# The last group of tokens: all first products, then the sums token block by token block; and the bias slabs ahead of the first weights

## The chip, the cores and the metric

The kernel runs on one core of one Trainium2 chip. The core has a matrix engine (TensorE, PE in the profile; its weight loads are a row of their own, PEld), a vector engine (DVE), an activation engine (ACT), GpSimd (POOL) and SyncE (SP), which in this kernel issues all transfers. The metric is device time in microseconds; less is better.

## The reference, cut to what matters

```python
# attention: B, H, S, D = 2, 8, 768, 64; keys kept: the first n_global = 8 and the last n_local = 96
scores = q @ k.T / sqrt(D) - slope[h] * dist        # dist depends on query - key alone
a = softmax(where(keep, scores, -1e9));  x = (a @ v) as (1536 tokens, 512)
# layer 0: 512 -> 2048 -> 512
h = x @ w_in;   g = max(h, 0) + log1p(exp(-|h|));   x = g @ w_out
# layer 1: 512 -> 2048 -> 512
h = x @ w_in;   g = h * clip(h + 3, 0, 6) / 6;      out = g @ w_out
```

The weights come in 64-bit floats; the result is 32-bit.

## The kernel before, in words

**Split products.** Every product of the two layers is made of three matmuls on a high and a low part of both factors (`matmul3`: low by high, high by low, high by high, in that order). So each weight and each activation exists as a pair (`wh`, `wl`; `gh`, `gl`; `xsh`, `xsl`).

**Weights.** The hidden dimension of 2048 is cut into 16 chunks of 128 for each layer. A chunk has two units, its slice of `w_in` and its slice of `w_out`, each a transfer of 512 KB (`unit_load`, L121) and a conversion to the pair (`unit_convert`): an absolute value on ACT (L140), a clamp on POOL (L143), three bit operations on DVE (L144, L147, L148), a copy that rounds to the high part (L103 on POOL beside the attention, L105 on ACT later) and a difference on DVE (L153). A converted chunk lives in one of 11 slots of four tiles; `weight_step(m)` loads ahead and converts the next m units.

**Attention.** It is done in 24 pairs k (12 blocks of 128 queries, half of the heads at a time). `att_s(k)` loads the block's q, k and v when it begins one, makes the scores on PE (L481), adds the bias and finds the row maxima on DVE (L487), takes the exponentials on ACT (L492), and scales rows on POOL (L380, after L377 and L378 on DVE). `att_t` transposes on PE (L513) and copies back on ACT (L515); `att_v` multiplies by v on PE (L531) and, when a block is complete, splits it into `xsh` and `xsl` (L538 on ACT, L539 on DVE). The scores alternate over two pairs of PSUM banks for the first five pairs.

**The bias.** For each head there is a slab of three parts of 128 by 128, made from `far`. The third part (the block's own diagonal, all that k = 0 and k = 1 use) is made by eight ACT instructions (L446); the first two parts, which the pairs from k = 2 on use too, by `bias_of(h)` on DVE (L449), one instruction for each head. A pair needs the slabs of four heads: even k heads 0 to 3, odd k heads 4 to 7.

**The start.** A loop over p = 0 to 4 issues `att_s` three pairs ahead, `att_v`, some matmuls on zeros (`warm_up`), `att_t` and weight units. Then `layers.run` interleaves the remaining pairs with the first phase of layer 0 (`half`): halves of 24 matmuls alternate between `hf` (first products) and `accf` (second products), each 128 by 256.

**The phases.** Each layer is done in phases of 6, 5 and 5 chunks; each phase goes over three groups of 512 tokens (G), and in a group over its chunks. `item` makes one chunk of one group: 12 matmuls of 512 columns for `h`, the activation (`split_g`: in layer 1 ACT L190, DVE L191, ACT L192, DVE L193), then for each of the four blocks m of 128 tokens three matmuls into `acc[m]`, a PSUM bank. After the last chunk of the last phase DVE adds each bank, times 1/6, to `part` (L305) and SP writes 128 rows of the result (L308, 256 KB).

**Order of instructions.** The framework plans the order on each engine by its own costs; an instruction that goes through `keep_in_program_order` is pinned behind the one traced before it on its engine. Pinned are all of PE's matmuls up to the end of the first phase, the ACT instruction L140 of a unit during that time, and every `bias_of`. SP issues in its planned order, and an issue that must wait holds those behind it.

**A second path.** `check_step` looks over q and k for values out of range (24 steps, spread over the last phase), and sets `flag`. Each engine loads it at the end (L759) and branches on it (L760) past a general path that does not run with these inputs.

Of the kernel before, what the change touches and what calls it, by code (L numbers as in the profile page):

```python
# [51 lines left out]
class Layers:  # L52
# [116 lines left out]

    def split_g(self, layer, hf, n):  # L170

        nc, mp = self.nc, self.mp
        gh = mp.tile([P, 512], F32R, tag="gh", name=f"gh{n}")
        gl = mp.tile([P, 512], F32R, tag="gl", name=f"gl{n}")
        t1 = self.tp.tile([P, 512], F32, tag="t", name=f"t1{n}")
# [88 lines left out]
    def item(self, layer, ph, G, s):  # L264
# [17 lines left out]
        for m in range(4):  # L282
# [23 lines left out]
            if last_ph:  # L306
                t0 = G * GB + m * P
                nc.sync.dma_start(out=self.out[t0:t0 + P, :], in_=pm)  # L308

    def release(self, layer, ph, chunks):  # L310
        base = layer * NCH + sum(PHASES[layer][:ph])
        self.free += [self.slot[base + s] for s in chunks]
# [5 lines left out]
    def run(self, att=None, spare_step=lambda: None):  # L318
# [34 lines left out]
        for layer in range(2):  # L353
            for ph, chunks in enumerate(PHASES[layer]):
                if layer == 0 and ph == 0:
                    continue
                for G in range(T // GB):
                    for s in range(chunks):
                        self.item(layer, ph, G, s)
                        if G == T // GB - 1:  # L360
                            self.release(layer, ph, (s,))
                        self.weight_step(2)
                        if layer == 1 and ph == len(PHASES[1]) - 1:
                            spare_step()
                            spare_step()
# [17 lines left out]
def fast_path(tc, ident, nf, counts, q, k, qt, kt, v, weights, out, flag):  # L383


    with ExitStack() as ctx, ExitStack() as actx:
# [60 lines left out]

        def bias_of(h):
            tc.keep_in_program_order(nc.vector.tensor_scalar(  # L449
                out=bias[:, h, 0:2, :], in0=far[:, 0:2, :], scalar1=-SLOPES[h] / SCALE, scalar2=None, op0=ALU.mult  # L450
            ))

# [3 lines left out]
        def att_s(k):  # L456
# [28 lines left out]
            for z in range(4):  # L485
# [5 lines left out]
                )  # L491
                nc.scalar.activation(pmz, pmz, AF.Exp, bias=nm[:, z:z + 1], scale=-1.0, accum_out=sm[:, z:z + 1])  # L492
            rs = ap_m.tile([P, 4], F32, tag="rs", name=f"rs{k}")
            softmax_rows(nc, sm, rs, [pm[:, z, 0:w] for z in range(4)])
# [122 lines left out]
        for p in range(LEAD):  # L617
            while step["s"] < min(p + AHEAD, quads):
                if step["s"] == 2:
                    layers.weight_step(1)  # L620
                    for h in range(H):
                        bias_of(h)
                att_step("s")
            att_step("v", p - V_LAG + 1)
            warm_up(FILL[p])
            for _ in range(2):
                att_step("t")
            layers.weight_step(LEAD_UNITS[p] - (p == 0))
        layers.run(Att, check_step)
# [178 lines left out]
```

## Time and profile before

| | us |
|---|---|
| time, median of 3 runs (lowest, highest) | 659.28 (657.86, 660.02) |
| the profiled execution: its time | 659.89 |
| the profiled execution: its span, from first to last instruction | 657.6 |
| TensorE busy in that span | 628.1 |
| DVE, ACT, POOL busy | 429.8, 375.4, 148.5 |
| mean granted TensorE clock | 0.988 |

The span is what the trace covers; the time includes 2.29 us around it. Busy times of different engines overlap.

### The profile page before, as it was taken

Reading aid. Unit: us, or ns where it says so; the run is one execution under the profiler, and the core shown is the slowest. Engines: PE = TensorE matmul, PEld = TensorE weight load, DVE = VectorE, ACT = ScalarE, POOL = GpSimd, SP = SyncE. Lnnn points to the kernel's source line nnn. Section 1 sums busy time; section 2 is a strip of 40 time slices with the busy share of each in tenths; the row PEclk is TensorE's granted clock in tenths of the full one; section 3 lists DMA queues with packets and bytes.
Section 4 is the critical chain, followed back from the end, with each engine's and each line's share of the span. In section 5 each row is a group of like instructions: output and inputs, shape, how many; then the busy total and the mean of one; then the engine's idle time right before and its main releaser. Section 6 shows DMA issues by size and latency. Waiting matters only on the chain.

```text
span 657.6 us, 9611 instructions
## 1 busy us (share of the span) xinstructions
PE 628.1 (96%) x3481; PEld 514.6 (78%) x3481; DVE 429.8 (65%) x902; ACT 375.4 (57%) x786; POOL 148.5 (23%) x192
## 2 busy tenths in 40 slices
PE   8587998999999999999999999999999999999995
PEld 4366887889999888877788888888877888888874
DVE  5897568654789999999998995225832333424242
ACT  5577778775587977867687852325675222212220
POOL 3575454531024132625200420000100000000000
PEclk9698999999999999999999999999999999999999
DMA  8452331101035233433311132000473000001011
GB/s 281 168 201 87 116 97 53 37 21 70 33 98 160 96 129 104 136 113 112 129 48 52 46 129 96 1 1 32 118 219 81 0 1 0 1 1 64 1 65 69
DMA packets 24937, 53.67 MB, mean 82 GB/s; under 512 B 2480, under 2 KB 8880, under 8 KB 24880
## 3 DMA queue, kind: packets, MB, share of 16 engines
q1 hardware_dynamic: 24880, 52.96, 24.8%
q8 instruction: 29, 0.48, 0.3%
q14 instruction: 28, 0.23, 0.1%
HBM read 49.81 MB, written 3.15 MB: 81 GB/s over the span
## 4 chain that ended last, share of the span: by engine, by line
PE 62%; DVE 19%; ACT 6%; DMA 4%; POOL 4%; issue 3%; SPq 0%; ACTq 0%; POOLq 0%; DVEq 0%
PE acc L201 22%; PE h L201 22%; PE accf L201 6%; PE hf L201 5%; DMA chk<-in_q 3%; DVE wa L147 2%; DVE wa L148 2%; POOL pm L380 2%; DVE w L153 2%; ACT pm L492 2%; PE ptp L513 2%; DVE pm L487 2%; PE s L481 2%; POOL wa L143 1%; DVE gl L193 1%
## 5 line engine op out<-in xcount | busy, mean ns | idle before, releaser
L201 PE MATMUL h<-xsh,w 128*128 128x512 f32 x624 | 170.3, 396 | 0.4 <-DVE t L187 0.4
L201 PEld LDWEIGHTS h<-xsh,w 128*128 128x128 f32 x624 | 116.7, 188 | 29.5 <-DVE t L187 1.6
L143 POOL TENSOR_SCALAR wa<-wa 128x512 f32<-128x512 f32 x56 | 76.3, 1368 | 240.2 <-ACT wa L140 239.9
L201 PE MATMUL acc<-w,gh 128*128 128x512 f32 x384 | 120.6, 395 | 0.0
L191 DVE SCALAR_TENSOR_TENSOR t<-t,h 128x512 f32<-128x512 f32 x48 | 32.9, 686 | 96.7 <-ACT t L190 96.7
L190 ACT ACTIVATE t<-h,three 128x512 f32<-128x512 f32 x48 | 33.0, 687 | 105.2 <-PE h L201 105.1
L201 PE MATMUL h<-xsl,w 128*128 128x512 f32 x312 | 87.8, 396 | 0.0
L193 DVE TENSOR_TENSOR gl<-t,gh 128x512 fp32r<-128x512 f32 x78 | 55.2, 708 | 47.3 <-ACT gh L192 47.0
L201 PEld LDWEIGHTS acc<-w,gh 128*128 128x128 f32 x384 | 72.0, 188 | 17.4
L201 PE MATMUL acc<-gh,w 128*128 128x512 f32 x240 | 78.9, 396 | 0.3 <-DVE part L297 0.2
L201 PE MATMUL acc<-w,gl 128*128 128x512 f32 x192 | 76.3, 397 | 0.8 <-ACT part L303 0.4
L192 ACT CAST gh<-t 128x512 fp32r<-128x512 f32 x78 | 48.3, 619 | 50.3 <-PE acc L201 24.3
L201 PEld LDWEIGHTS h<-xsl,w 128*128 128x128 f32 x312 | 58.5, 188 | 14.1
L380 POOL TENSOR_SCALAR pm<-pm,rs 128x256 f32<-128x256 f32 (+1 forms) x96 | 51.0, 549 | 44.5 <-DVE rs L378 33.2
L201 PE MATMUL accf<-ghf,w 128*128 128x256 f32 x288 | 59.6, 291 | 0.6 <-ACT ghf L192 0.6
L492 ACT ACTIVATE pm<-pm,nm 128x256 f32<-128x256 f32 (+1 forms) x96 | 46.0, 480 | 16.5 <-DVE nm L487 16.3
L201 PEld LDWEIGHTS acc<-gh,w 128*128 128x128 f32 x240 | 44.9, 188 | 11.9 <-DVE part L297 0.6
L201 PEld LDWEIGHTS accf<-ghf,w 128*128 128x128 f32 x288 | 47.3, 191 | 2.2 <-issue 1.2
L201 PE MATMUL acc<-gl,w 128*128 128x512 f32 x120 | 47.5, 396 | 0.0
L153 DVE TENSOR_TENSOR w<-wa,w 128x512 fp32r<-128x512 f32 x56 | 38.9, 696 | 9.2 <-ACT w L105 8.3
L201 PE MATMUL hf<-xsh,w 128*128 128x256 f32 x288 | 44.8, 286 | 0.0
L201 PEld LDWEIGHTS acc<-w,gl 128*128 128x128 f32 x192 | 36.0, 188 | 11.0 <-DVE gl L193 1.7
(105 smaller groups left out, 989.2 us busy)
## 6 DMA issues: line engine op xcount, KB each, us to landing
raw<-in_w2i SPq DMA_DIRECT2D x16, 512.0 KB, 3.3
raw<-in_w2o SPq DMA_DIRECT2D x16, 512.0 KB, 3.3
raw<-in_w1i SPq DMA_DIRECT2D x14, 512.0 KB, 3.6
raw<-in_w1o SPq DMA_DIRECT2D x12, 512.0 KB, 3.3
V<-in_v SPq DMA_DIRECT2D x12, 256.0 KB, 2.9
chk<-in_q SPq DMA_DIRECT2D x12, 256.0 KB, 3.3
chk<-in_k SPq DMA_DIRECT2D x12, 256.0 KB, 2.8
out_x<-part SPq DMA_DIRECT2D x12, 256.0 KB, 2.1
```

What stands on the lines that cost most here:

```text
L143: nc.gpsimd.tensor_scalar(out=a, in0=a, scalar1=W_HI, scalar2=W_LO, op0=ALU.min, op1=ALU.max)
L147: nc.vector.scalar_tensor_tensor(out=ai, in0=hi, scalar=-2 ** 30, in1=ai, op0=ALU.bitwise_and, op1=ALU.bitwise_or)
L148: nc.vector.scalar_tensor_tensor(out=ai, in0=lo, scalar=29, in1=ai, op0=ALU.logical_shift_right, op1=ALU.bitwise_or)
L153: nc.vector.tensor_tensor(out=wl, in0=a, in1=r32(wh), op=ALU.subtract)
L190: nc.scalar.activation(t1, hf, AF.Relu, bias=self.three[:, 0:1])
L191: nc.vector.scalar_tensor_tensor(out=t3, in0=t1, scalar=6.0, in1=hf, op0=ALU.min, op1=ALU.mult)
L192: nc.scalar.copy(gh, t3)
L193: nc.vector.tensor_tensor(out=gl, in0=t3, in1=r32(gh), op=ALU.subtract)
L201: return self.nc.tensor.matmul(out, lhsT=a, rhs=b, start=start and z == 0, stop=stop and z == len(seq) - 1, **kw)
L380: nc.gpsimd.tensor_scalar(out=t, in0=t, scalar1=rs[:, j:j + 1], scalar2=0.0, op0=ALU.mult, op1=ALU.add)
L481: layers.ordered(lambda: nc.tensor.matmul(ps[j][:, a, 0:nsl, :], lhsT=qT[n][hp, 2 * e + a, :], rhs=kT[hp, 2 * e + a, ks, :], start=True, s ...
L492: nc.scalar.activation(pmz, pmz, AF.Exp, bias=nm[:, z:z + 1], scale=-1.0, accum_out=sm[:, z:z + 1])
```

## The change

Two things are changed. In the start, `bias_of` takes a range of heads: heads 0 to 3 are done as soon as `far` exists, heads 4 to 7 inside `att_s(0)` behind its four L487, and the third pair's `att_s` no longer has a weight unit and eight `bias_of` in front of it; both units of p = 0 come at the end of p = 0. In the last phase of layer 1, the last group no longer goes through `item`: `last_items` makes the `h` and `g` of all five chunks first (the pairs of `g` in a free weight slot, two of its four tiles), and then for each block m of 128 tokens all five chunks' matmuls, the addition and the transfer; the last block in two halves of 256 columns. The remaining four `check_step` calls come behind the first chunk of that group.

```diff
--- before.py
+++ after.py
@@ -167,11 +167,10 @@
             self.unit_convert(x)
             self.done += 1
 
-    def split_g(self, layer, hf, n):
+    def split_g(self, layer, hf, n, where=None):
 
         nc, mp = self.nc, self.mp
-        gh = mp.tile([P, 512], F32R, tag="gh", name=f"gh{n}")
-        gl = mp.tile([P, 512], F32R, tag="gl", name=f"gl{n}")
+        gh, gl = where or [mp.tile([P, 512], F32R, tag=f"g{z}", name=f"g{z}{n}") for z in "hl"]
         t1 = self.tp.tile([P, 512], F32, tag="t", name=f"t1{n}")
         t3 = self.tp.tile([P, 512], F32, tag="t", name=f"t3{n}")
         if layer == 0:
@@ -307,6 +306,39 @@
                 t0 = G * GB + m * P
                 nc.sync.dma_start(out=self.out[t0:t0 + P, :], in_=pm)
 
+    def last_items(self, ph, G, spare_step):
+
+
+        nc, part = self.nc, self.part[G]
+        g, W = [], []
+        for s in range(PHASES[1][ph]):
+            W.append(self.W[NCH + sum(PHASES[1][:ph]) + s])
+            wih, wil = (t.rearrange("p (k c) -> p k c", k=KC) for t in W[s][0:2])
+            h = self.h_bank(f"hz{s}")
+            for call in self.matmul3(
+                h, [((wih[:, c], wil[:, c]), (self.xsh[G][:, c, :], self.xsl[G][:, c, :])) for c in range(KC)], True, True
+            ):
+                call()
+            wp, t = self.free.pop(0)
+            where = [wp.tile([P, CW], F32R, tag=f"w{i}_{t}", name=f"g{i}_{s}") for i in range(2)]
+            g.append(self.split_g(1, h, f"z{s}", where))
+            for _ in range(4):
+                spare_step()
+        for m in range(4):
+            acc = self.bank(self.acc_tags[m], f"accz{m}")
+            t0 = G * GB + m * P
+            ms = slice(m * P, (m + 1) * P)
+            for cs in (slice(0, 512),) if m < 3 else (slice(0, 256), slice(256, 512)):
+                for s, (gh, gl) in enumerate(g):
+                    pair = ((gh[:, ms], gl[:, ms]), (W[s][2][:, cs], W[s][3][:, cs]))
+                    for call in self.matmul3(acc[:, cs], [pair], s == 0, s == len(g) - 1, skip_group_check=True):
+                        call()
+                pm = part[:, m, cs]
+                nc.vector.scalar_tensor_tensor(
+                    out=pm, in0=acc[:, cs], scalar=1.0 / 6.0, in1=pm, op0=ALU.mult, op1=ALU.add
+                )
+                nc.sync.dma_start(out=self.out[t0:t0 + P, cs], in_=pm)
+
     def release(self, layer, ph, chunks):
         base = layer * NCH + sum(PHASES[layer][:ph])
         self.free += [self.slot[base + s] for s in chunks]
@@ -355,6 +387,9 @@
                 if layer == 0 and ph == 0:
                     continue
                 for G in range(T // GB):
+                    if layer == 1 and ph == len(PHASES[1]) - 1 and G == T // GB - 1:
+                        self.last_items(ph, G, spare_step)
+                        continue
                     for s in range(chunks):
                         self.item(layer, ph, G, s)
                         if G == T // GB - 1:
@@ -445,10 +480,13 @@
         for h in range(H):
             nc.scalar.mul(bias[:, h, 2, :], far[:, 2, :], -SLOPES[h] / SCALE)
 
-        def bias_of(h):
-            tc.keep_in_program_order(nc.vector.tensor_scalar(
-                out=bias[:, h, 0:2, :], in0=far[:, 0:2, :], scalar1=-SLOPES[h] / SCALE, scalar2=None, op0=ALU.mult
-            ))
+        def bias_of(hs):
+            for h in hs:
+                tc.keep_in_program_order(nc.vector.tensor_scalar(
+                    out=bias[:, h, 0:2, :], in0=far[:, 0:2, :], scalar1=-SLOPES[h] / SCALE, scalar2=None, op0=ALU.mult
+                ))
+
+        bias_of(range(H // 2))
 
         pms, pTs = {}, {}
         s_tags = [(ps_s, f"s{j}") for j in range(2)]
@@ -490,6 +528,8 @@
                     scale=-SCALE, scalar=3.0e38, op0=ALU.add, op1=ALU.min, accum_out=nm[:, z:z + 1],
                 )
                 nc.scalar.activation(pmz, pmz, AF.Exp, bias=nm[:, z:z + 1], scale=-1.0, accum_out=sm[:, z:z + 1])
+            if k == 0:
+                bias_of(range(H // 2, H))
             rs = ap_m.tile([P, 4], F32, tag="rs", name=f"rs{k}")
             softmax_rows(nc, sm, rs, [pm[:, z, 0:w] for z in range(4)])
             if e == KC // 2 - 1 and 1 <= i < NB - 1:
@@ -616,16 +656,12 @@
         warm_up(WARM)
         for p in range(LEAD):
             while step["s"] < min(p + AHEAD, quads):
-                if step["s"] == 2:
-                    layers.weight_step(1)
-                    for h in range(H):
-                        bias_of(h)
                 att_step("s")
             att_step("v", p - V_LAG + 1)
             warm_up(FILL[p])
             for _ in range(2):
                 att_step("t")
-            layers.weight_step(LEAD_UNITS[p] - (p == 0))
+            layers.weight_step(LEAD_UNITS[p])
         layers.run(Att, check_step)
 
 
```

## Rows read from the trace of the kernel before

**Rows 1.** The page, its head and part 1: busy us, share, instructions.
```profile
span 657.6 us, 9611 instructions
PE 628.1 (96%) x3481; PEld 514.6 (78%) x3481; DVE 429.8 (65%) x902; ACT 375.4 (57%) x786; POOL 148.5 (23%) x192
```
**Rows 2.** Windows: stretch, length, busy us by engine, PEclk, DMA share, GB/s.
```profile
9.10:61.60 52.50, 36.77 (x296) 26.86 (x294) 42.22 (x143) 36.84 (x115) 32.88 (x57) 0.90 0.56 194
9.10:13.20 4.10, 4.05 (x23) 1.91 (x23) 0.74 (x7) 3.81 (x16) 2.85 (x9) 1.00 1.00 360
13.20:23.10 9.90, 1.92 (x16) 1.08 (x14) 9.73 (x20) 1.36 (x4) 3.46 (x5) 0.85 0.97 347
...
61.60:158.00 96.40, 92.61 (x835) 81.69 (x837) 61.88 (x201) 70.97 (x190) 41.26 (x73) 0.98 0.19 57
158.00:627.00 469.00, 467.55 (x2221) 384.12 (x2218) 310.21 (x513) 258.34 (x461) 73.02 (x53) 1.00 0.23 73
...
21.00:30.50 9.50, 6.21 (x28) 4.39 (x30) 8.30 (x39) 6.91 (x26) 4.09 (x9) 0.50 0.32 112
```
**Rows 3.** Timeline of PE: start us, us, operation, count, idle before and releaser.
```profile
7.96 1.56 PE L481 MATMUL s<-kT,qT 64*128 64x256 f32 x8 [0.32 <-PE s L481]
...
24.29 2.42 PE L481 MATMUL s<-kT,qT 64*128 64x256 f32 x8 [9.18 <-DVE nm L487]
...
61.61 0.58 PE L201 MATMUL accf<-glf,w 128*128 128x256 f32 x1 [3.06 <-DVE glf L193]
```
**Rows 4.** Timeline of DVE, from 5.7 to 23.5 us.
```profile
5.76 0.61 DVE L444 SCALAR_TENSOR_TENSOR far<-gfar,nf,far 128x384 f32<-128x384 f32 x1
7.34 0.29 DVE L487 CUSTOM_DVE_ANT_0 pm<-s,bias 128x128 f32<-128x128 f32 x1 [0.97 <-ACT bias L446]
...
13.17 0.67 DVE L496 COPY kT<-gk 128x128 f32<-128x128 f32 x1 [1.57 <-PE s L481]
...
20.31 1.69 DVE L449 TENSOR_SCALAR bias<-far 128x256 bf16<-128x256 f32 x8
...
23.13 0.41 DVE L487 CUSTOM_DVE_ANT_0 pm<-s,bias 128x256 f32<-128x256 f32 x1
```
**Rows 5.** Timeline of ACT, from 9.5 to 24 us.
```profile
9.55 0.38 ACT L492 ACTIVATE pm<-pm,nm 128x128 f32<-128x128 f32 x1
...
11.42 0.67 ACT L140 ACTIVATE part<-part 128x512 f32<-128x512 f32 x1 [0.23 <-DMA part<-in_w1i]
...
23.59 0.51 ACT L492 ACTIVATE pm<-pm,nm 128x256 f32<-128x256 f32 x1 [7.44 <-DVE nm L487]
```
**Rows 6.** Timeline of SP: issues of the first weights and of block 2.
```profile
4.94 0.91 SPq L121 DMA_DIRECT2D part<-in_w1i  x2
...
8.59 0.55 SPq L410 DMA_DIRECT2D qT<-in_qt  x1
```
**Rows 7.** Timeline from 646.9 us: the end of the last group.
```profile
646.91 0.69 DVE L193 TENSOR_TENSOR gl<-t,gh 128x512 fp32r<-128x512 f32 x1 [0.69 <-ACT gh L192]
...
647.65 0.19 PEld L201 LDWEIGHTS acc<-w,gl 128*128 128x128 f32 x1 [0.52 <-DVE gl L193]
...
648.66 2.78 DVE L305 SCALAR_TENSOR_TENSOR part<-acc,part 128x512 f32<-128x512 f32 x4 [1.06 <-PE acc L201]
...
650.09 0.62 PE L201 MATMUL acc<-w,gh 128*128 128x512 f32 x2
```
**Rows 8.** Line 760, by queue: duration ns min/median/max, first and last start us.
```profile
L760 SPq EVENT_SEMAPHORE  x8: 17/17/17, 655.3 to 656.2; - x8
L760 POOLq COMPARE_BRANCH  x1: 45/45/45, 630.0 to 630.0; - x1
L760 POOLq EVENT_SEMAPHORE  x1: 17/17/17, 632.5 to 632.5; - x1
...
L760 SPq COMPARE_BRANCH  x1: 50/50/50, 651.9 to 651.9; - x1
```
**Rows 9.** The chain that ended last: start us, us, what, count.
```profile
161.87 2.84 PE accf L201 x24
...
641.28 2.80 PE acc L201 x12
644.07 0.72 PE h L201 x3
```

## The prediction

> **What bounds the kernel now.** I read the page's head first: TensorE is busy for 628.1 of 657.6 us [rows 1], so at most some 29.5 us can be had without fewer matmuls, and the question is where these gaps lie. Windows by stage answer it. From 158 to 627 us PE is busy for 467.55 of 469 us, from 61.6 to 158 us for 92.61 of 96.4, but from 9.1 to 61.6 us for 36.77 of 52.5 only: 15.73 us idle, half of all [rows 2]. The reader is to see that the start is where time lies loose, and that whatever is won there passes to the end, because the long middle is one full PE queue.
>
> PE's own timeline shows where: the scores of k = 2 are made at 7.96 us, and those of k = 4 start at 24.29 us, after 9.18 us of waiting for DVE's L487, which has to read the banks of k = 2 first [rows 3]. L487 of k = 2 runs at 23.13 us, some 13.6 us after its scores were there (7.96 + 1.56 = 9.52), just behind the eight slabs of L449 at 20.31 to 22.00 us [rows 4]. ACT starves with it: 7.44 us of idle before the exponentials of k = 2 at 23.59 us [rows 5]. The slabs were pinned behind the first unit's conversion, and that unit arrives only at 11.42 us [rows 5]. But DVE itself is not idle from 13.2 to 23.1 us: 9.73 of 9.9 us busy with conversions [rows 2]. So the gap of PE is not one of DVE, and that decides how much of it can come back.
>
> The end is a chain of another kind: `gl` of the last chunk ends at about 647.6 us, PE waits 0.52 us for it, then come four additions of 0.695 us each (2.78 in all) with one PE bank after the other, so that the last addition ends at 651.44 us although PE ends at 650.71 [rows 7]. From there to the end of the span it is 6.16 us, of which SP's branch, 651.9 to 655.3 us, is 3.4 [rows 8].
>
> **The change part by part: the start.** One slab costs 1.69 / 8 = 0.21 us on DVE [rows 4].
>
> Heads 0 to 3 (0.85 us) move to 6.37 us, when `far` is ready (5.76 + 0.61), in front of L487 of k = 0, which waited 0.97 us for ACT's slabs until 7.34 [rows 4]. 6.37 + 0.85 = 7.22: hidden by ACT's slabs, and if those were earlier it would cost up to 0.85.
>
> Heads 4 to 7 (0.85 us) go behind L487 of k = 0 and push L487 of k = 1 by as much. ACT takes the exponentials of k = 1 from 9.55 us on [rows 5]; L487 of k = 1 then begins at about 9.05 instead of 8.2 and its first row maxima are there at 9.35. So this is hidden too, by ACT's exponentials of k = 0; without that cover it is 0.85.
>
> Removed are the first unit and the slabs from in front of `att_s(2)`. L487 of k = 2 (four of about 0.35 us by their spacing, 0.41 each [rows 4]) can start at about 10.2, behind the scaling of k = 0, instead of 23.13. PE can then start the scores of k = 4 right after the transposes of k = 1, at about 15 to 16 us instead of 24.29.
>
> The transfers move as well. Before, SP issued the first five units from 4.94 us on and block 2's q at 8.59 [rows 6]; now q, k and v of the next block go first, three transfers of 256 KB. With 360 GB/s flowing [rows 2] that makes the first unit 0.79 MB / 360 = 2.2 us later: 13.6 instead of 11.4. Its ACT instruction is pinned, behind the copies of k = 0's transposes, and exponentials are queued behind it. ACT has four exponentials of k = 2 (0.51 each [rows 5]) and these copies between 11.2 and some 13.7, so this wait is about nothing; at most it is 2.2 us.
>
> How much comes back? The work on DVE from 9.1 to 61.6 us remains: 42.22 us, less the 1.69 of slabs, which now lie outside or in an earlier hole. Idle on DVE there: 52.5 - 42.22 = 10.28 us, 3.36 of it between 9.1 and 13.2 [rows 2]. The upper bound, DVE never idle, is 10.28 plus the 0.85 of slabs that go into the hole at 6.4: 11.1 us. The lower bound is 0: the conversions, now later, hold up the products that need them, and PE waits at the first `accf` instead (it waits 3.06 us for DVE there already, at 61.61 [rows 3]). I take the early hole in full, since L487 of k = 2 and k = 3 are ready work for it, the 0.85, and a third of the other 6.9 us, since the later holes are waits from engine to engine that are filled only in part: 3.36 + 0.85 + 2.3 = **6.5 us**. The half-speed spell is inside this: from 21 to 30.5 us the granted clock is 0.50, 1.2 GHz, after the long gap [rows 2], and without the gap it should not come there.
>
> **The end.** The number of matmul columns is unchanged: 60 for `h` and 60 for the sums, at 2.80 / 12 = 0.233 us each [rows 9]; thirty halves at 2.84 / 24 = 0.118 us [rows 9] cost 3.55 us instead of 3.50. The wait of 0.52 us for `gl` falls away, since behind the last `h` PE has 12 matmuls of block 0 that need only earlier chunks, 2.80 us, and the way from `h` to `gl` takes 644.79 to 647.60 [rows 7, 9], 2.81: a wait of 0 to 0.1 remains. The queue of four additions dissolves, one per 3.5 us; only the last half, 256 columns, stands behind PE. No row shows that addition at 256 columns; bounds are 0.28 (L487 at 128) and 0.695 (L305 at 512), and I take 0.41, L487 at 256 [rows 4, 7]. PE's end moves to 650.71 - 0.52 = 650.19, the last addition's end to about 650.65, a gain of 0.8 us. Against it: both halves lie in one bank. If PE may not write the bank while DVE reads its first half, PE waits some 0.5 us and the gain is 0.3. No row shows a bank that is written and read at once; I take 0.5.
>
> (The Trainium skill, page "PSUM — Partial Sum Buffer", section "PSUM bank collisions raise a hardware error", says that two engines on one bank collide even at different columns, and that software must order them. That speaks against the halves: by it the end's gain would be 0.3, and the total 0.2 us smaller. The trace has no such case.)
>
> The last transfer is half as long, and SP's and DVE's branches at the end come with less in flight: POOL's branch at 630.0 resumed after 2.5 us, SP's after 3.4 us with the results under way [rows 8]. Bounds are 0 and 0.9; I take 0.5. (The Trainium skill, "Runtime: NRT & Kernel Launch", section "Instruction fetch mechanics", has a taken branch fetch its target by DMA. By that rule it would be nearer 0.9; the two rows agree with it.) End: **1.0 us**.
>
> **Sum.** 6.5 + 1.0 = 7.5 us off the profiled 659.89, 652.4; that execution is 0.6 us above the median of the runs, so against 659.28 it is **651.8 us**.
>
> **The rivals.** (a) *All of PE's gap returns.* If DVE is kept full to 61.6 us, the start gives 10 to 11 us and the end 1.0 to 1.5: 647.5. For it: weights are needed only when `hf` and `accf` begin, so conversions can wait; against it: DVE's work there is fixed. (b) *DVE hands it back.* The conversions, 2.2 us later and behind more attention work, make `hf` and `accf` wait; the start gives 1 to 2 us, the end 0.5: 657.3. For it are DVE's 9.73 of 9.9 us [rows 2] and the wait at 61.61 [rows 3]. (c) *Slower: half speed where PE is full.* The spell of clock 0.50 now falls mostly on PE's gap. If the late conversions make PE wait as long as 9 us beyond 30 us, where it is otherwise nearly full, a spell of 9.5 us costs up to half of that, 4.75 us, beside the wait of 9 us itself: 659.28 - 7.5 + 13.8 = 665.5. It decides against the change once wait and spell together exceed 7.5 us, so from a further wait of about 2.8 us on, if a whole spell follows it. Against it: the 3.06 us at 61.61 are there before too, so it takes a new wait as long, and before then no wait of PE behind conversions shows.
>
> **How the numbers follow.** A measurement of this kernel can tell about 0.3%, 2 us, from no change. Forecast 0.55 (own range 649.0 to 654.5), (a) 0.15, (b) 0.22, (c) 0.08. The range leaves out the far half of (a), (c), and the upper half of (b): 647.0 to 657.3. Faster by over 0.3%: 0.55 + 0.15 + half of (b) = 0.81; within: 0.11; slower: 0.08.
>
> **What would show it.** In the profile after: L449 in two groups of four, at about 6.4 and 8.2 us; L487 of k = 2 near 10.2; the scores of k = 4 near 15.5, with no PE wait of 9 us in front; clock 1.00 until 60 us; the first `accf` around 55 instead of 58 to 61. At the end 60 `h` matmuls without a break, additions one by one, the last with 256 columns, and SP's branch under 3.4 us. The prediction is wrong if PE waits for conversions (L153) before 60 us, if ACT stands before L140 for over 1 us, or if the stretch from 61.6 us to the end changes its length by more than the end's 1.0, since the planner orders everything anew.

## The result: 1.6% faster, three gains where two were forecast

| | before | after |
|---|---|---|
| median of the runs | 659.65 us (657.86 to 660.17, 4 runs) | 648.76 us (648.15 to 649.24, 4 runs) |
| ratio, 95% interval | | 0.9839 [0.9818, 0.9861] |
| profiled execution: time, span | 659.89, 657.6 us | 649.05, 647.1 us |

The forecast was 651.8 us (own range 649.0 to 654.5, whole range 647.0 to 657.3). The result lies in the whole range and just outside the forecast's own: 10.5 us came off the span where 7.5 were reckoned.

Where they came off is found by matching the same events in both traces (the instruction that makes the same piece of `g`, the addition that ends the same result) and taking the differences of their times. From 76 to 468 us the changed kernel is 8.0 to 8.1 us ahead, almost without a step. Between the events at 468.0 and 512.5 us of before it gains another 1.5 us. From there to 600 us it gains nothing, and in the last group 0.95. So 8.0 + 1.5 + 0.95 = 10.45.

The windows of the changed kernel that answer to those of [rows 2]; the columns are length, busy time of PE, PE's weight loads, DVE, ACT and POOL, then granted clock, DMA share and GB/s:

```profile
9.10:54.00 44.90, 36.58 (x293) 26.35 (x293) 38.40 (x135) 34.99 (x108) 35.40 (x55) 0.96 0.67 223
9.10:13.20 4.10, 3.53 (x19) 1.75 (x18) 2.50 (x19) 4.10 (x20) 2.51 (x8) 1.00 1.06 398
13.20:23.10 9.90, 9.19 (x77) 6.06 (x74) 8.52 (x36) 9.68 (x32) 8.05 (x14) 1.00 0.75 268
32.00:42.00 10.00, 6.48 (x59) 5.36 (x57) 9.93 (x32) 6.21 (x20) 9.83 (x14) 0.99 0.65 187
42.00:54.00 12.00, 11.23 (x89) 9.22 (x89) 8.56 (x26) 8.35 (x20) 7.79 (x12) 0.87 0.39 129
150.00:619.00 469.00, 468.27 (x2229) 385.43 (x2226) 312.43 (x518) 258.91 (x462) 70.86 (x53) 1.00 0.23 74
```

The first row ends at the event that ended the 9.10:61.60 of before. PE does the same work (36.6 us) but is idle for 8.32 us instead of 15.73. From 13.2 to 23.1 us, where it had 1.92 us of work, it now has 9.19, and the clock stays at 1.00. The largest piece of what is left lies from 32 to 42 us: there DVE and POOL are both full and PE has 3.5 us of idle time.

PE's timeline of the changed kernel, for [rows 3]; start, duration, engine, line, operation, and in brackets the idle time before it and its releaser:

```profile
7.88 1.33 PE L519 MATMUL s<-kT,qT 64*128 64x256 f32 x8 [1.32 <-DVE nm L525]
15.56 1.13 PE L519 MATMUL s<-kT,qT 64*128 64x256 f32 x8
42.03 1.09 PE L553 MATMUL ptp<-ident,pm 128*128 128x128 f32 x4 [2.83 <-ACT pT L555]
53.31 0.39 PE L200 MATMUL accf<-ghf,w 128*128 128x256 f32 x1 [0.44 <-ACT ghf L191]
54.04 0.39 PE L200 MATMUL accf<-glf,w 128*128 128x256 f32 x1 [0.34 <-DVE glf L192]
```

The scores of k = 4 start at 15.56 us with no wait in front (24.29 and 9.18 before), and the first `glf` costs 0.34 us where it cost 3.06. DVE and ACT, for [rows 4, 5]:

```profile
6.23 0.90 DVE L485 TENSOR_SCALAR bias<-far 128x256 bf16<-128x256 f32 x4
7.89 0.89 DVE L485 TENSOR_SCALAR bias<-far 128x256 bf16<-128x256 f32 x4
9.62 0.43 DVE L525 CUSTOM_DVE_ANT_0 pm<-s,bias 128x256 f32<-128x256 f32 x1
13.40 1.24 ACT L140 ACTIVATE part<-part 128x512 f32<-128x512 f32 x2
38.86 0.51 ACT L530 ACTIVATE pm<-pm,nm 128x256 f32<-128x256 f32 x1 [3.12 <-DVE nm L525]
```

The slabs run in two groups of four, the row maxima of k = 2 at 9.62 us, and ACT takes the first units at 13.40 without waiting. The end, for [rows 7, 8]:

```profile
637.11 0.69 DVE L337 SCALAR_TENSOR_TENSOR part<-accz,part 128x512 f32<-128x512 f32 x1 [0.67 <-PE accz L200]
638.90 0.42 DVE L337 SCALAR_TENSOR_TENSOR part<-accz,part 128x256 f32<-128x256 f32 x1 [1.10 <-PE accz L200]
639.38 1.85 PEld L200 LDWEIGHTS accz<-w,g 128*128 128x128 f32 x15 [0.72 <-DVE part L337]
639.38 2.05 PE L200 MATMUL accz<-w,g 128*128 128x256 f32 x15 [0.52 <-DVE part L337]
641.47 0.42 DVE L337 SCALAR_TENSOR_TENSOR part<-accz,part 128x256 f32<-128x256 f32 x1 [2.14 <-PE accz L200]
```

and its line 796 by queue (count, duration in ns, first and last start):

```profile
L796 SPq EVENT_SEMAPHORE  x8: 17/17/17, 645.2 to 645.7; - x8
...
L796 SPq COMPARE_BRANCH  x1: 50/50/50, 642.3 to 642.3; - x1
```

PE stands still for 0.52 us in front of the second half, until DVE has read the first half of the same bank. The last addition ends at 641.89; to the end of the span it is 5.21 us (6.16 before), SP's branch in it 2.9 us (3.4).

### The profile page after: what moved, and what is told of

The parts are those of the page before. It is cut to its first block, busy times and chain, and to the rows that moved or that the text cites. A ratio compares the mean times of both kernels' runs of the same rounds, so it can differ in the third digit from the quotient of the medians.

```text
span 647.1 us, 9643 instructions
## 1 busy us (share of the span) xinstructions
PE 624.8 (97%) x3495; PEld 513.8 (79%) x3496; DVE 428.9 (66%) x903; ACT 375.1 (58%) x786; POOL 151.0 (23%) x192
## 4 chain that ended last, share of the span: by engine, by line
PE 68%; DVE 16%; ACT 7%; POOL 3%; DMA 3%; issue 2%; SPq 0%; ACTq 0%; DVEq 0%
PE acc L200 25%; PE h L200 24%; PE accf L200 6%; PE hf L200 5%; ACT pm L530 3%; PE accz L200 2%; PE hz L200 2%; DVE wa L147 2%; DVE wa L148 2%; PE ptp L553 2%; DVE w L153 2%; POOL wa L143 1%; POOL pm L415 1%; DVE pm L525 1%; DVE part L296 1%
## 5 line engine op out<-in xcount | busy, mean ns | idle before, releaser
L200 PE MATMUL h<-xsh,w 128*128 128x512 f32 x584 | 159.3, 396 | 0.4 <-DVE t L186 0.4
L200 PEld LDWEIGHTS h<-xsh,w 128*128 128x128 f32 x584 | 109.2, 188 | 27.6 <-DVE t L186 1.6
L200 PE MATMUL acc<-w,gh 128*128 128x512 f32 x344 | 108.0, 395 | 0.0
L200 PE MATMUL h<-xsl,w 128*128 128x512 f32 x292 | 82.4, 395 | 0.0
L192 DVE TENSOR_TENSOR gl<-t,gh 128x512 fp32r<-128x512 f32 x73 | 51.8, 709 | 43.1 <-ACT gh L191 42.8
L189 ACT ACTIVATE t<-h,three 128x512 f32<-128x512 f32 x43 | 29.5, 686 | 87.6 <-PE h L200 87.4
L200 PEld LDWEIGHTS acc<-w,gh 128*128 128x128 f32 x344 | 64.5, 188 | 15.7
L200 PE MATMUL acc<-w,gl 128*128 128x512 f32 x172 | 68.0, 396 | 0.0
L200 PEld LDWEIGHTS h<-xsl,w 128*128 128x128 f32 x292 | 54.8, 188 | 13.2
L153 DVE TENSOR_TENSOR w<-wa,w 128x512 fp32r<-128x512 f32 x56 | 39.2, 700 | 9.7 <-ACT w L105 8.4
L140 ACT ACTIVATE wa<-raw 128x512 f32<-128x512 f32 x53 | 35.5, 673 | 13.7 <-DVE w L153 6.4
```

Of the source, the lines that this page charges most:

```text
L140: first = nc.scalar.activation(a, raw.bitcast(F32)[:, :, 1], AF.Abs)
L153: nc.vector.tensor_tensor(out=wl, in0=a, in1=r32(wh), op=ALU.subtract)
L189: nc.scalar.activation(t1, hf, AF.Relu, bias=self.three[:, 0:1])
L192: nc.vector.tensor_tensor(out=gl, in0=t3, in1=r32(gh), op=ALU.subtract)
L200: return self.nc.tensor.matmul(out, lhsT=a, rhs=b, start=start and z == 0, stop=stop and z == len(seq) - 1, **kw)
```

## The experiments

All ratios are against the kernel before, run on the same chip. "Shift" is a kernel's time at a matched event minus that of before (its first profile), at 76 us, behind the first sums. Profiles with the same start differ in it: the three with the start of before have 0, +0.6 and +0.8 us, the four with the changed start -7.9 to -9.0. So a shift is good to about 1 us. A half-speed spell below is a stretch in which the granted clock is about 0.50, 1.2 GHz.

**The two halves of the change, apart.** `front_only` is the kernel before with the edits of the start, `end_only` with those of the end:

```diff
 # front_only
+        bias_of(range(H // 2))
...
+            if k == 0:
+                bias_of(range(H // 2, H))
...
-                if step["s"] == 2:
-                    layers.weight_step(1)
-                    for h in range(H):
-                        bias_of(h)
...
-            layers.weight_step(LEAD_UNITS[p] - (p == 0))
+            layers.weight_step(LEAD_UNITS[p])
 # end_only
+                    if layer == 1 and ph == len(PHASES[1]) - 1 and G == T // GB - 1:
+                        self.last_items(ph, G, spare_step)
+                        continue
```

> The start's edits alone (slabs of heads 0 to 3 in front of the first scores, 4 to 7 behind the row maxima of k = 0, first unit's conversion behind the fill matmuls), the end as before. Theory A, the three gains are separate (start 8.0, check stretch 1.5, end 0.95 us) and the check stretch's belongs to no edit, but differs from execution to execution: 8.0 us faster, with 0 to 1.5 more by chance, and PE's waits in the stretch of the check's loads (470 to 500 us) differ between profiles of one and the same order. Rival B, the 1.5 us come from the start (the check's loads now meet other transfers): 9.5 us faster in every run and no wait over 0.4 us there. Rival C, they come from the end's edit: 8.0 us faster, and the three waits stand there as before, 8 us earlier.

> The end's edit alone, the start as before. A: 0.9 to 1.0 us faster, with 0 to 1.5 more by chance. B: 1.0 us faster, and the three waits in the stretch of the check's loads stand as before. C: 2.5 us faster, none of the three waits. In all of them: 60 matmuls of h without a break, 0.5 us of waiting in front of the second half's matmuls, last result's transfer 1.8 us, SP's last branch 2.9 us instead of 3.4.

`front_only`: 648.81 us, ratio 0.9853 [0.9831, 0.9876]; shift -8.4, and 1.5 more in the stretch of the check's loads. `end_only`: 657.65 us, 0.9981 [0.9968, 0.9993]; shift +0.8, 0.7 less in that stretch, and the tail as forecast (0.52 us of wait, last addition to span end 5.08 us). Theory C falls: the end's edit alone keeps 0.8 of the 1.5 us of that stretch. Between A and B the two runs don't decide, see below.

**Which edit of the start does it?** The slabs alone, and the unit alone:

```diff
 # bias_only: bias_of as in front_only, and
                 if step["s"] == 2:
                     layers.weight_step(1)
-                    for h in range(H):
-                        bias_of(h)
 # unit_only
                 if step["s"] == 2:
-                    layers.weight_step(1)
                     for h in range(H):
                         bias_of(h)
...
-            layers.weight_step(LEAD_UNITS[p] - (p == 0))
+            layers.weight_step(LEAD_UNITS[p])
```

> Only the slabs are moved; the first unit's conversion stays in front of the scores of k = 2, so that its transfers are issued ahead of the next block's. Theory 1, what cost the time was only that the slabs were pinned behind the first unit: 7 to 8 us faster, row maxima of k = 2 near 10 us, scores of k = 4 near 15.5. Rival 2, the unit's place counts by itself (its conversion takes DVE and ACT ahead of the attention's work, and its transfers go ahead of the next block's): 1 to 4 us faster, scores of k = 4 at 18 us or later.

> Only the first unit's conversion is moved, behind the first fill matmuls; all eight slabs stay in front of the scores of k = 2, now pinned behind the scaling of k = 1. Theory 1: the slabs run at about 11.5 to 13.2 us, row maxima of k = 2 near 13.3, scores of k = 4 near 17; 5.5 to 7.5 us faster, since 1.7 us of slabs lie once more where DVE is wanted. Rival 2: 7 to 8 us faster, as the unit's place is nearly all of it. Rival 3, the slabs' place is nearly all of it: 1 to 3 us faster.

`bias_only`: 654.29 us, 0.9932 [0.9907, 0.9956], shift -3.1. `unit_only`: 650.15 us, 0.987 [0.9845, 0.9895], shift -8.9. By these shifts theory 1 falls and rival 2 holds: the slabs alone give a third, and the unit alone gives all of it, though the slabs stay in front of k = 2 (at 11.33 us there, row maxima at 13.25). The ratios say it less sharply: 4.5 us for the slabs alone, 8.6 for the unit alone, 9.7 for both (`front_only`). The profiled execution of `unit_only` is also the fastest of its four (647.8 us) and has no half-speed spell, so that slabs in front of k = 2 cost nothing is not shown. Moreover, `bias_only` did put the row maxima of k = 2 at 9.57 us, as theory 1 wants. PE's timeline shows where it waited afterwards:

```profile
18.34 2.08 PE L484 MATMUL s<-kT,qT 64*128 64x256 f32 x8 [2.44 <-DMA kT<-in_kt]
...
55.92 0.58 PE L201 MATMUL accf<-ghf,w 128*128 128x256 f32 x1 [3.55 <-ACT ghf L192]
57.58 0.58 PE L201 MATMUL accf<-glf,w 128*128 128x256 f32 x1 [1.08 <-DVE glf L193]
```

There are two places: the keys of the next block, which stand behind five weight units in the queue (landing at 18.2 us, in the changed kernel at 10.0), and the first sums. PE's order is the same in all these kernels, so the scores of k = 10, the last ones in front of the first sums, tell the two apart. They start in before, `bias_only` and the changed kernel at:

```profile
55.46 1.14 PE L481 MATMUL s<-kT,qT 64*128 64x256 f32 x8
50.20 1.13 PE L484 MATMUL s<-kT,qT 64*128 64x256 f32 x8
50.71 1.13 PE L519 MATMUL s<-kT,qT 64*128 64x256 f32 x8
```

In `unit_only` it is 50.17 us. So by then either edit alone has the whole gain, some 5 us, and the late keys are made up for. What `bias_only` lacks at 76 us it loses at the first sums.

**The order of the transfers.** The same kernel, with the block's loads first:

```diff
                 if step["s"] == 2:
+                    load_block(2)
+                    load_values(1)
                     layers.weight_step(1)
 # att_s
-                if n + 1 < B * NB:
+                if n + 1 < B * NB and k != 2:
                     load_block(n + 1)
-                load_values(n)
+                if k != 2:
+                    load_values(n)
```

> As the run with only the slabs moved, but the q, k and v of the next block are issued ahead of the five weight units, while the first unit's conversion keeps its place in front of the scores of k = 2. Theory, it is the order of the transfers that the slabs alone left open: k of the block lands near 10 us instead of 18.2, the scores of k = 4 start at 15 to 16 us and not at 18.3, and it is 7 to 9.5 us faster than the kernel before. Rival, it is the conversion's instructions on DVE and ACT in front of the attention's: the scores of k = 4 stay at 17.5 us or later, 4 to 5.5 us faster.

`bias_loads`: 655.77 us, 0.9946 [0.9927, 0.9966], shift -2.7: no gain. The keys land at 10.6 us, as meant, but now the unit is late, and ACT stands for it with the exponentials of k = 2 queued behind:

```profile
12.58 0.67 ACT L140 ACTIVATE part<-part 128x512 f32<-128x512 f32 x1 [1.57 <-DMA part<-in_w1i]
```

The scores of k = 4 begin at 19.12 us. My theory of the transfers falls: while the unit's instruction stands in front of k = 2, one of the two loads is late, whichever goes first. Nor does it matter at k = 10, whose scores start at 50.12 us here. The waits at the first sums stay (4.0 and 1.7 us from start to start).

**The first sums: POOL's queue.** DVE and POOL of `bias_only` in front of those waits:

```profile
49.79 3.10 POOL L380 TENSOR_SCALAR pm<-pm,rs 128x256 f32<-128x256 f32 x4 [1.29 <-DVE rs L378]
52.86 0.61 POOL L103 TENSOR_SCALAR w<-part 128x512 fp32r<-128x512 f32 x1
...
53.51 0.69 DVE L153 TENSOR_TENSOR w<-part,w 128x512 fp32r<-128x512 f32 x1 [1.19 <-POOL w L103]
54.12 1.10 DVE L188 TENSOR_TENSOR t3f<-t3f,t2f 128x512 f32<-128x512 f32 x1
```

and POOL of the changed kernel:

```profile
50.02 1.06 POOL L103 TENSOR_SCALAR w<-part 128x512 fp32r<-128x512 f32 x1 [3.80 <-DVE rs L413]
51.06 3.27 POOL L415 TENSOR_SCALAR pm<-pm,rs 128x256 f32<-128x256 f32 x4
```

The cast of the seventh unit stands behind the four scalings of k = 9 in the one, in front of them in the other. DVE's subtraction L153 waits for that cast, and behind L153 stands the g that PE needs. The planner chose the place; no line of the change speaks of it. In the kernel before it is as in `bias_only`, and there DVE's own timeline has the wait (a row that the prediction did not use):

```profile
55.09 3.17 POOL L380 TENSOR_SCALAR pm<-pm,rs 128x256 f32<-128x256 f32 x4 [2.38 <-DVE rs L378]
58.24 0.61 POOL L103 TENSOR_SCALAR w<-part 128x512 fp32r<-128x512 f32 x1
...
58.88 0.69 DVE L153 TENSOR_TENSOR w<-part,w 128x512 fp32r<-128x512 f32 x1 [1.42 <-POOL w L103]
```

Three kernels force the place, in both directions:

```diff
 # unit_convert (end(pin) issues the cast, pinned if asked, and the subtraction)
-        self.cast(wh, a)
-        nc.vector.tensor_tensor(out=wl, in0=a, in1=r32(wh), op=ALU.subtract)
+        if x == 6 and self.beside:
+            self.late = end
+        else:
+            end()
 # att_s in bias_pool and before_pool; the scalings of k = 9 are pinned too
+            if k == 9:
+                layers.late()
             softmax_rows(nc, sm, rs, [pm[:, z, 0:w] for z in range(4)])
 # att_s in after_late
             softmax_rows(nc, sm, rs, [pm[:, z, 0:w] for z in range(4)])
+            if k == 9:
+                layers.late(tc.keep_in_program_order)
```

> The run with only the slabs moved, and one thing more: POOL's cast of the seventh weight unit (L103), which that run and the kernel before have behind the four scalings of k = 9, is put in front of them, where the changed kernel has it. Theory, the first sums of the feed-forward wait because DVE's subtraction for that unit (L153) waits for POOL and the g of the first item stands behind it: the waits of 3.55 and 1.08 us at 56 to 57.6 us fall under 1.5 together, the half-speed spell behind them goes, and the gain over the kernel before grows from 4.4 to 7.5 to 9 us. Rival, POOL's order is a mere sign of an earlier delay: the waits stay, 4 to 5 us faster than before as that run.

> The kernel before with nothing changed but that cast of POOL's, put in front of the scalings of k = 9. Theory: the wait of 3.06 us for the first glf shrinks under 1 us and the half-speed spell at 61 to 64.6 us goes; 3 to 4.5 us faster than before, although slabs and unit are where they were, so that nearly half of the change's gain is this one place in POOL's queue. Rival: 0 to 1 us faster, since conversions are as late as they were.

> The changed kernel with that cast put behind the scalings of k = 9, as the kernel before has it. Theory: the waits in front of the first sums grow from 0.8 to 3 to 5 us, and it is 3 to 5 us slower than the changed kernel, some 652 to 653.5 us. Rival: the scalings are done in time anyway, under 1 us slower.

| start as in | ratio, the run with the cast moved | shift, cast behind | shift, cast in front |
|---|---|---|---|
| the kernel before | `before_pool` 0.9970 [0.9956, 0.9983] | 0 | -1.8 |
| slabs moved | `bias_pool` 0.9881 [0.9855, 0.9907] | -3.1 | -6.9 |
| slabs and unit moved | `after_late` 0.9863 [0.9840, 0.9885] | -5.2 | -8.1 |

Read across, the cast's place is worth 1.8 to 3.8 us in each row (by the ratios 2.0, 3.4 and 1.6). Part of these differences is there before the cast runs; counted from the scores of k = 10 to those of k = 12, just behind the first sums, it is 2.3, 2.9 and 2.1 us. Read down, taking the slabs out from behind the unit gives 3.1 to 5.1 us, and moving the unit in addition 1.2 to 2.1, which is hardly above what a shift is good to. So theory 1 was in large part right after all; `bias_only` seemed to refute it because it kept the cast where it was, while `unit_only`, which also takes the slabs out from behind the unit, got the other place by the planner's choice. `before_pool` shortens the wait of before, and `after_late` makes it come back, by the very instruction; first `before_pool`, then `after_late`:

```profile
56.21 1.00 POOL L103 TENSOR_SCALAR w<-part 128x512 fp32r<-128x512 f32 x1 [2.99 <-DVE part L147]
...
59.43 0.39 PE L207 MATMUL accf<-ghf,w 128*128 128x256 f32 x1 [1.30 <-ACT ghf L198]
60.76 0.39 PE L207 MATMUL accf<-glf,w 128*128 128x256 f32 x1 [0.94 <-DVE glf L199]
```

```profile
53.10 0.61 POOL L103 TENSOR_SCALAR w<-part 128x512 fp32r<-128x512 f32 x1
...
53.74 0.69 DVE L154 TENSOR_TENSOR w<-part,w 128x512 fp32r<-128x512 f32 x1 [1.42 <-POOL w L103]
55.04 1.10 DVE L198 TENSOR_TENSOR glf<-t3f,ghf 128x512 fp32r<-128x512 f32 x1
...
56.19 0.39 PE L206 MATMUL accf<-glf,w 128*128 128x256 f32 x1 [2.22 <-DVE glf L198]
```

The mechanism holds, the sizes less well. `bias_pool` (651.89 us) gains 7.8 us as expected (1.19%), but waits of 1.67 and 0.95 us and a clock of 0.66 from 55 to 60 us are left. `before_pool` (657.83 us) gains 2 us, not 3 to 4.5, though its spell at 61 us is gone. `after_late` is at 650.87 us, not 652 to 653.5: against the changed kernel it loses 2.1 us by the medians and 1.6 by the ratios, whose intervals overlap, and its wait is 2.22 us, not 3 to 5. Its shift is 2.9 us worse, but the profiled execution was the slowest of its four.

**The end.** The second half in a bank of its own, and no halves:

```diff
 # other_bank
             for cs in (slice(0, 512),) if m < 3 else (slice(0, 256), slice(256, 512)):
+                if cs.start:
+                    acc = self.h_bank("accy")
 # one_block
-            for cs in (slice(0, 512),) if m < 3 else (slice(0, 256), slice(256, 512)):
+            for cs in (slice(0, 512),):
```

> The changed kernel, with the last half of the last block summed in a bank of its own (one of h, long free). Theory, PE may not write a bank that DVE reads: the wait of 0.52 us in front of the second half goes, the last addition ends 0.5 us earlier after the start of the last group's sums, about 0.5 us less, which the times alone can hardly tell. Rival, the wait is one for the pieces of the result or for DVE itself: it stays, and nothing changes.

> The changed kernel without the halves: the last block of 128 tokens is summed, added and sent whole. Theory, by the rows of the changed kernel: without the bank's wait the sum ends at about 640.65 us instead of 641.43, the addition takes 0.69 instead of 0.42 and ends at 641.35 instead of 641.89, the transfer lands in 2.05 instead of 1.83 us; so 0.3 us less in all, and the halves in one bank are no gain. Rival, the halves pay: the transfer of 256 KB takes SP's last branch back to 3.4 us, and it is 0.2 to 0.5 us slower.

`other_bank`: 647.75 us, 0.9828 [0.9813, 0.9843]. `one_block`: 648.37 us, 0.9833 [0.9818, 0.9848]. The times don't tell these from the changed kernel (0.9839); the ends of the traces do.

```profile
637.64 1.96 PE L200 MATMUL accy<-w,g 128*128 128x256 f32 x15
...
639.64 0.42 DVE L339 SCALAR_TENSOR_TENSOR part<-accy,part 128x256 f32<-128x256 f32 x1 [1.37 <-PE accy L200]
```

The first half's sums end at 637.81 us there, as DVE's addition of them starts at 637.85. The second half runs on without a break and ends 1.79 us later, where the changed kernel needs 2.56 (638.87 to 641.43): 0.77 us, the wait of 0.52 and 0.25 more until PE is back at its pace. `one_block` starts its one last addition at 640.77 us. Set against the matched events at 588 us (it is 0.26 us later there), the last addition ends 0.69 us earlier than with the halves, and the tail behind it is about 0.1 us longer. So in one bank the halves cost about 0.6 us. In two banks they are 0.2 to 0.3 us better than the whole block (0.08 in the addition's end, the rest in the tail), which is no more than the tails of the kernels with a half block last differ among themselves (5.0 to 5.2 us); a gain is not shown.

**The stretch of the check's loads.** In this stretch q and k are loaded and squared on ACT, for the flag. The kernel before once more, unchanged:

> The kernel before, unchanged, profiled a second time. If the 1.5 us in the stretch of the check's loads (470 to 506 us) are chance, this profile has other waits there than the three of the first (0.81, 0.49 and 0.61 us between starts), none or fewer; if they belong to the kernel before, the same three stand there again. The start's events should lie within 0.6 us of the first profile's.

From a `gl` to a result slab (468.0 to 512.5 us of before) the same instructions in the same order on PE, DVE and ACT take, in the fourteen profiles: 44.44 us (before), 43.83 (`before_again`), 43.72 (`end_only`), 44.24 (`before_pool`); and 42.88 to 43.55 in the ten others, 42.92 in the changed kernel. `before_again` ran once, in 660.3 us; all three waits stood there again, at the same matmuls but shorter: 0.41, 0.43 and 0.49 us between starts, where they were 0.81, 0.49 and 0.61. `before_pool` has all three as well, `end_only` the last two; of the ten others four have the last, at 0.36 to 0.55 us (one of them the second too, at 0.37), and six none, the changed kernel among them. So part is chance, up to 0.7 us between profiles of the same start; yet the waits belong mostly to the old start, and the four that have it are the four longest. In before, six of the check's loads issued from 479.7 to 484.6 us land after 3.4 to 4.1 us; in the changed kernel, those at that place after 2.7 to 4.1. ACT's squares wait for them, and the next g behind. Why they land later there is open.

**A version that beats both.** The bank of its own, and the conversions that keep DVE full from 34 to 38.3 us put one step later:

```diff
-LEAD_UNITS = (2, 1, 1, 1, 1)
-HALF_UNITS = (1, 1, 0, 0, 0, 1, 0, 1, 0, 1, 0, 1)
+LEAD_UNITS = (2, 1, 1, 1, 0)
+HALF_UNITS = (1, 1, 1, 0, 0, 1, 0, 1, 0, 1, 0, 1)
```

> The changed kernel with the last half in a bank of its own and with the sixth, seventh and eighth weight units each converted one step later (behind the first, second and third half item instead of the lead's last step, the first and the second). Theory, DVE's conversions from 34 to 38.3 us make the row maxima at 38.3 us late, ACT stands 3.12 us for them with the next copy behind, and so PE waits 2.4 to 2.8 us at 42 us: the wait falls under 1 us, and it is 1.5 to 2.5 us faster than the run with the bank alone, about 645.5 us. Rival, the conversions are only put off to where the first sums need the sixth unit: PE waits there by as much more, within 0.7 us of the run with the bank alone.

`eased`: 646.53 us, 0.9797 [0.9778, 0.9816], against 0.9839 [0.9818, 0.9861] of the changed kernel. Its shift is -10.0 although its first loads land late. The wait at 42 us shrank, but not under 1 us, as the window and PE's timeline show:

```profile
32.00:42.00 10.00, 7.66 (x77) 6.46 (x73) 8.89 (x30) 6.32 (x20) 9.04 (x13) 1.00 0.57 193
```

```profile
41.55 0.63 PE L555 MATMUL ptp<-ident,pm 128*128 128x128 f32 x4 [1.63 <-ACT pT L557]
```

DVE is no longer full there, PE has 1.2 us more work in the window, and the first sums come without a new wait (0.34 us). The intervals of `eased` and the changed kernel just miss each other. The gain over the bank alone is 1.2 us by the medians and 2.0 by the ratios, whose intervals just overlap ([0.9813, 0.9843] for `other_bank`).

## Why the prediction came out so

The total came 3 us better than forecast and stayed inside the range, but not term by term: the start's term was 1.5 us too small, 1.5 us more stand in no term, and the end's total fits with both of its parts wrong. So the hit is in part luck.

**What held.** That the long middle passes on what the start wins: 8.0 us at 76 us are 8.0 at 468. That PE's 9 us of waiting go, and where the events come: slabs at 6.23 and 7.89 us (6.4 and 8.2 forecast), row maxima of k = 2 at 9.62 (10.2), scores of k = 4 at 15.56 (15.5), first `glf` sums at 54.0 (55), no wait of ACT in front of L140, SP's branch under 3.4 us. The 60 matmuls of `h` are not without a break, as forecast: the first 20 stand between sums of the group before, and 40 come in a row, from 617.36 us on.

**The start: 6.5 was mis-sized, 8.0 measured, and its yardstick was too narrow.** Of the 8.0 us, 4.75 are there at the scores of k = 10 (50.71 against 55.46 us); the other 3.3 come at the first sums, where the waits shrink from 0.55 and 3.06 us to 0.44 and 0.34 and the half-speed spell behind them (61.1 to 64.6 us in before) is gone. I counted what DVE's idle time could give back. The early hole, taken in full at 3.36 us, still has 1.60 of its 4.1 us idle, so it gave 1.76. Over the whole stretch DVE's idle time fell from 10.28 to 6.50 us, 3.8; the other 3.8 us (42.22 - 38.40) is busy time that no longer lies between these events: 1.69 of slabs, of which I had counted 0.85, and 2.1 of other work. That other work is hardly work put elsewhere, since apart from the eight slabs both windows hold 135 instructions of DVE; it is mostly the same number of instructions in less busy time, which the sum took as fixed. Of the 8.0 us, `after_late` gives back 2.9 (2.1 from k = 10 to k = 12): they hang on POOL's cast before or behind four scalings, a place that the sum did not have. I had read the wait of 3.06 us at 61.61 [rows 3] as a sign that DVE is short of time, for rival (b); but DVE stood for POOL itself, 1.42 us in front of L153.

**Rival (a)** comes near by its number (647.5), not by its mechanism: 8.32 of PE's 15.73 us of idle time are still there, 3.52 of them from 32 to 42 us, where DVE and POOL are full. What stands there comes near the first sign of being wrong, PE waiting for conversions before 60 us: PE's wait of 2.83 us at 42.03 us comes from ACT, which stood 3.12 us for row maxima that DVE made behind conversions, and in `eased` it is 1.63 us with the conversions put later.

**The unit's move was reckoned as a cost of 0 to 2.2 us.** By the shifts it is a gain of 1.2 to 2.1, hardly clear of what they differ by. The delay itself was too large in the sum: the unit's first transfer lands at 11.99 us, 0.6 later than before and not 2.2. As long as the unit's instruction stands in front of k = 2, either the next block's keys are late (2.44 us of PE's wait in `bias_only`) or the unit is (1.57 us of ACT's in `bias_loads`), but neither delay is what costs, since both kernels have made it up by k = 10. They lose at the first sums, with POOL's cast in front too (1.67 and 0.95 us of wait in `bias_pool`); why they wait more there is open.

**The clock.** "1.00 until 60 us" was wrong: a half-speed spell stands at 41.7 to 45.1 us (0.87 in the window 42:54), beside the wait of 2.83 us. Rival (c) named this mechanism; it had a wait of 9 us and a spell of 9.5 for it, and here a wait of 2.83 and a spell of 3.4 us leave the gain standing.

**The end: 1.0 forecast, 0.95 measured, but not 0.5 and 0.5.** Set against the events at 600 us, the last addition ends only 0.03 us earlier than before (641.89 + 9.52 = 651.41 against 651.44): the wait for `gl` and the queue of additions are gone, and the break of 0.77 us in the halves takes it all back, worse than my lower bound of 0.3. `other_bank` gets 0.8 us (640.06 + 10.58 = 650.64), the upper bound as worked out. The Trainium skill, page "PSUM — Partial Sum Buffer", section "PSUM bank collisions raise a hardware error", says that two engines may not be on one bank at once and that software has to order them. The trace agrees as far as the order goes: PE waits on a semaphore for DVE's 0.42 us addition.

The tail gave 0.95 instead of 0.5, from 6.16 to 5.21 us. SP's branch has 0.5 of it (3.4 to 2.9 us), as taken in the sum. Another 0.3 lies behind the branch, in no term: in before SP resumes at 655.35 us but then waits for the last result, which lands at 655.82, and goes on at 655.84; in the changed kernel the last result lands at 643.75, before SP resumes at 645.19. Part may be chance, for the tail is 5.7 to 6.5 us in the eight profiles with four results queued, 5.3 with one block last and 5.0 to 5.2 in the five with a half block last. The Trainium skill, page "Runtime: NRT & Kernel Launch", section "Instruction fetch mechanics", says that a taken branch out of the instructions already loaded has its target fetched by DMA. The 0.9 that I had named for that rule was not reached: the branch takes 3.3 to 3.5 us in the eight profiles, 2.7 to 2.9 in the five. That the fetch itself was what waited is not shown by these runs.

**The 1.5 us at 468 to 512 us** were in no term. The prediction named the sign ("changes by more than the end's 1.0"), but the cause that it gave, a new order, is not it: the order there is the same.

## What to carry to other kernels

When a wait names an engine, look at what that engine itself waited for: "PE <- DVE" was DVE <- POOL, and one cast in front of or behind four scalings in POOL's queue was worth 2 to 3 us. An edit whose gain depends on where a planner then puts other work has to be tried with that place held fixed, or one reads the place's worth as the edit's. A wait early in a chain may be made up for later, so it pays to look at an event behind it before putting a price on it. Halving the last block to shorten the tail cost more than it saved here with both halves in one PSUM bank; in two banks it cost nothing, and a gain was too small to show.

## What the hardware showed that I had not expected

PE, with 15 matmuls ready for columns 256 to 511 of a bank, waited 0.52 us for DVE's read of columns 0 to 255 of it, and lost 0.77 us in all; in another bank it lost nothing. The wait itself was in the prediction, the other 0.25 us were not. The wait is one on a semaphore, so the runs show the program's order and its price, not what the chip would do without it.

Where the half-speed spell falls is not fixed by the kernel's start. The changed kernel and `other_bank` have the same start, with the same instructions in the same order; the spell is at 40 to 45 us in the one and at 30 to 35 in the other, as these windows of the two show (granted clock third from the right):

```profile
30.00:35.00 5.00, 3.25 (x33) 2.93 (x34) 5.00 (x17) 3.00 (x10) 4.83 (x8) 1.00 0.86 256
40.00:45.00 5.00, 2.97 (x14) 2.60 (x16) 2.89 (x6) 3.65 (x10) 4.92 (x8) 0.68 0.44 147
```

```profile
30.00:35.00 5.00, 3.90 (x27) 3.60 (x28) 5.00 (x17) 2.27 (x8) 4.83 (x7) 0.66 0.79 272
40.00:45.00 5.00, 2.57 (x21) 1.88 (x21) 3.41 (x11) 4.14 (x13) 3.78 (x7) 1.00 0.54 168
```

The shift at 76 us differs by 0.9 us between them. `one_block`, with the same start again, has two spells, at 33.0 and at 43.3 us. `eased`, whose longest waits of PE behind 30 us are 1.77 and 1.63 us, has no spell at all, and neither has `unit_only`, with a wait of 2.20 us at 42.23. So a wait of PE alone does not tell where a spell comes.
